# A two-part kernel (chunked delta rule, then PReLU feed-forward): reordering the second chunk's two steps, and starting the third block inversion earlier

## The chip, the cores and the metric

One core of a Trainium2 chip. TensorE (PE) multiplies into PSUM, VectorE (DVE), ScalarE (ACT) and GpSimd (POOL) work on SBUF tiles, SyncE (SP) issues nearly all DMAs. The metric is the device time of one execution in microseconds. Four runs of the kernel before took 666.1, 666.4, 667.12 and 671.37 us; their median is 666.76 us.

## The reference

```python
B, H, S, D = 4, 8, 768, 48
k_n = k / (norm(k) + 1e-06)
for t in range(S):                       # state: (B, H, D, D), zero at first
    y[:, :, t] = q_t @ state
    v_old = state^T k_t
    state += beta_t * outer(k_t, v_t - v_old)
x = y as (B*S, H*D)                      # 3072 x 384
h = x @ w_in                             # 384 x 2048
g = max(h, 0) + alpha * min(h, 0)
out = g @ w_out                          # 2048 x 384
```

All of it is float32. The first part is a recurrence over 768 tokens, the second a feed-forward layer over 3072 rows.

## The kernel before

**Steps.** The sequence is cut into 12 chunks of 64 tokens, and the four batches into two pairs. A step n is one chunk of one pair, so there are 24 steps, and steps 2c and 2c+1 make chunk c. The 128 partitions hold 64 tokens of two batches. For a step the kernel needs the Gram matrix of its keys (grams, L418), the inverse of a triangular 64x64 matrix for each head, and then the products with the running state: through_state (L754), solve (L785), outputs (L797) and next_state (L811). to_ffn (L833) turns the step's rows for the feed-forward layer.

**Before a step.** load_early (L139) brings a step's keys into one of three key buffers (a fourth at the start is lent by k_late). squares (L343) squares them on ACT and sums them on DVE; weigh (L352) takes the root on ACT, the reciprocal on DVE and two small products on POOL; flips (L383) transposes keys or queries on PE and copies them out on ACT. grams writes its products with weights by two DVE instructions (L430) into the tiles same and right, and keep (L467) copies half of right to same, on POOL for nearly all steps up to 9 and on ACT from step 10.

**The inverse.** Four steps are inverted together. turn_in (L492) transposes their Gram blocks by four DVE transposes (L489). eliminate (L501) then clears one triangle on POOL (L506, L510) and does 30 elimination steps on DVE, two instructions each (L516, L522), and back (L528) transposes the results by eight L489 into the tiles turned and inverse. That inverts the 32x32 blocks: 39 pieces, and four more where turn_in is part of it. The 64x64 inverse is put together in each step: place (L622) copies to diag and inv on ACT (L642, L648, and L659 for weights), between_1 (L702) and between_2 (L716) are the two products. For the first four steps 16x16 blocks are inverted first and joined by cross (L582), a generator of two halves: the first is 64 small matmuls (L593) and an ACT copy (L598) for a step, the second 96 (L603, L610) and three DVE instructions (L617, L619).

**The feed-forward layer.** ffn_in(c) (L922) makes 8 groups of 12 matmuls (L931) for chunk c, 48 parts in all; after each group ACT makes the negative part (L941) and DVE two instructions (L943). Two PSUM tiles, p_ffn, take turns. ffn_out(c) (L961) has 32 parts (L974). Both weights are converted at the start from words fetched into staging space: L209 fetches, L225 and L226 on ACT and L235 and L240 on DVE convert.

**Order.** The order of every engine is written out by hand: what the program issues first runs first on its engine, and an instruction that waits holds up all that stands behind it on that engine. weave (L1290) interleaves generators in equal shares, so that a feed-forward pass runs between the small products of the steps. The parts of the program around the change are, in order:

- first_chunk (L1417), steps 0 and 1; at its end it issues the loads of the late keys and values of steps 2 to 4, and fetches of weights.
- second_pair (L1555), steps 2 and 3, beside ffn_in(0) and 22 pieces of the conversion; alongside (L1552) issues so many parts of the one and pieces of the other. It also does squares, flips, weigh and grams of steps 4 to 7.
- A weave (L1628) of ffn_in(1), the conversion, statics (L1463: squares, weigh, flips, grams of steps 8 and 9) and the first 15 pieces of eliminate(1), the second inversion.
- A weave (L1637) of ffn_out(0), the last pieces of conversion and the rest of eliminate(1).
- Three parts of ffn_out(1), then prelude (L1642, step 4 made ready) and catch_up (L1654, grams of steps 10 and 11, flips and weights of 11 and 12) beside eight parts of ffn_out(1).
- attention(4) and attention(5) (L1307), each beside 11 parts of ffn_out(1) and 13 pieces of eliminate(2), the third inversion (L1697). turn_in(2) is issued all at once by keep(11) (L478).
- From step 6 on (L1712) each step has three stretches (L1691), whose shares of the next inversion stand in PIECES_OF and TURNS.

Of the kernel before, what the change touches and what calls it, by code (L numbers as in the profile page):

```python
# [43 lines left out]
def kernel(  # L44
# [363 lines left out]
    def now(pieces):  # L408
        for x in pieces:
            x()  # L410
# [56 lines left out]
    def keep(n):  # L467

        m, j = n // NJ, n % NJ
        for t in range(2):  # L470
            own = slice(64 * t + HB, 64 * t + C)
            if n < FIRST + NJ and n != NJ - 1:
                nc.gpsimd.tensor_copy(out=same[m][own, j], in_=right[n % EARLY][own, 1:])
            elif n < NJ and t == 0:
                nc.vector.tensor_copy(out=same[m][own, j], in_=right[n % EARLY][own, 1:])
            else:
                nc.scalar.copy(same[m][own, j], right[n % EARLY][own, 1:])
        if j == NJ - 1 and m in (0, 2):  # L478
            for _ in turn_in(m):
                pass  # L480

# [18 lines left out]

    def eliminate(m):  # L501

        if m not in (0, 2):
            yield from turn_in(m)
        r = block[m]
        nc.gpsimd.affine_select(  # L506
# [115 lines left out]
    def place(n, parts=(0, 1, 2, 3), by_vector=False):  # L622
        for _ in placing(n, parts, by_vector):
            pass
# [927 lines left out]
    def alongside(products, pieces, *gens):  # L1552
        weave((part(first_in, products), products), (part(convert_on, pieces), pieces), *gens)

    def second_pair():  # L1555

        n = 2
        both, x = (n, n + 1), NJ
        halves = [cross(0, slice(i * H, i * H + H), edge, half_way) for i in both]
        squares(x)  # L1560
        alongside(4, 2)
        for h in halves:
            next(h)
        flips(x, n)
        load_early(x + NKE)
        load_q(n + 2)
        squares(x + 1)
        alongside(5, 2)
        next(halves[0])
        flips(x + 1, n + 1)  # L1570
        load_early(x + 1 + NKE)
        load_q(n + 3)
        now(weigh(x))
        place(n, (0,))
        alongside(4, 2)
        next(halves[1])
        now(weigh(x + 1))
        place(n + 1, (0,))
        alongside(4, 2)
        for i in both:  # L1580
            now(between_1(i))
        now(grams(x))
        squares(x + 2)
        alongside(7, 3, (chain(*(placing(i, (1, 2, 3)) for i in both)), 6))
        for i in both:
            now(between_2(i))
        now(grams(x + 1))
        for i in both:
            scale_v(i)
        flips(x + 2, N)  # L1590
        load_early(x + 2 + NKE)
        now(weigh(x + 2))
        alongside(5, 3)
        y = ps_big()
        pieces = []
        for i in range(2):
            pieces += through_state(n + i, None, y[:, :, i * G * D : (i + 1) * G * D])
        now(pieces)
        squares(x + 3)
        alongside(5, 3)  # L1600
        y = ps_big()
        pieces = []
        for i in range(2):
            pieces += solve(n + i, y[:, :, i * G * D : (i + 1) * G * D])
        now(pieces)
        now(grams(x + 2))
        flips(x + 3, N)
        load_early(x + 3 + NKE)
        now(weigh(x + 3))
        alongside(5, 2)  # L1610
        pieces = []
        for i in both:
            y = ps_big()
            pieces += outputs(i, y[:, :, 0 : G * D]) + next_state(i, y[:, :, G * D : 2 * G * D])
        now(pieces)
        for i in both:
            load_late(i + 2)
            load_v(i + 3)
        alongside(5, 2)
        for i in both:  # L1620
            to_ffn(i)
        now(grams(x + 3))
        alongside(IN_PARTS - 44, 1)

    second_pair()
    fetch_out(len(stages))
    blocks, SOON, LAST = eliminate(1), 15, 6
    weave(  # L1628
        (part(conv_out, PARTS_OUT - 10 - LAST), PARTS_OUT - 10 - LAST), (ffn_in(1), IN_PARTS - 4),
        (statics(2 * NJ, FIRST + 3), 2 * (FIRST + 4 - 2 * NJ) + 1), (part(blocks, SOON), SOON),  # L1630
    )
    flips(FIRST + NJ, NJ)
    flips(N, NJ + 1)
    prep(FIRST + NJ)
    load_early(FIRST + NJ + NKE)
    load_q(NJ + 2)
    weave(  # L1637
        (conv_out, OUT_PARTS // 2), (part(blocks, WHOLE + PIECES - SOON), WHOLE + PIECES - SOON),
        (ffn_out(0, True), OUT_PARTS),
    )  # L1640

    def prelude(n):  # L1642
        place(n, (0,))
# [7 lines left out]
        place(n + 1, (0,))  # L1651
        yield

    def catch_up():  # L1654
        for n in range(FIRST + NJ, EARLY + NJ):
            now(grams(n))
            flips(n + 1, N)
            squares(n + 1)
            yield
            now(weigh(n + 1))  # L1660
            load_early(n + 1 + NKE)
            yield

    late = ffn_out(1)
    few, rest = OUT_PARTS // 4, 11
    for _ in part(late, OUT_PARTS - few - 2 * rest + 1):
        pass
    weave((prelude(NJ), 3), (catch_up(), 2 * (EARLY - FIRST), 0.1), (part(late, few), few))

    def feed_forward():  # L1670
        for c in range(2, FAST_IN):
# [22 lines left out]
        gens += [(part(blocks, share), share, 0.3), (each(later), len(later), soon)]  # L1694
        weave(*[x for x in gens if x[1] > 0])

    blocks, share = eliminate(2), WHOLE // 3  # L1697
    for n in range(NJ, JOINED):
        extra = [] if n == NJ else [(weight_sums(0, 0, 3), 3)]
        weave(  # L1700
# [3 lines left out]
        )  # L1704

    assert next(late, None) is None
    PIECES_OF = {JOINED: (2, 3, 2 * PIECES), JOINED + 1: (4, 4, 7)}
    TURNS = [(3, 3, 4), (3, 3, 4), (4, 4, 4), (0, 5, 6)]
    FILL = {JOINED: (8, 12, 12), JOINED + 1: (10, 12, 10), JOINED + 2: (8, 10, 12)}
    FILLS = [(12, 10, 12), (12, 18, 12)]  # L1710
# [78 lines left out]
```

## Time and profile before

| what | us |
|---|---|
| median of four runs | 666.76 |
| the profiled execution's own time | 669.61 |
| its span, first to last instruction | 667.9 |
| PE busy | 646.4 |
| DVE busy | 492.2 |
| ACT busy | 264.3 |
| mean granted clock of PE | 0.995 |

The profile is of one execution. A row of its timeline has the start, the duration, the engine, the line of the kernel, the operation and tiles, and the idle time before it with what ended that idle time. Matmuls are pipelined: the end of one is modelled, so that the time from the start of one burst to the start of the next tells what a burst costs, and the busy time says somewhat too much. SPq is the queue of DMA issues on SP; "issue" is time in which the engine waited for nothing that the profile shows.

### The profile page before, as it was taken

The numbers are of one execution on the slowest core, as the hardware profiler recorded it, in microseconds if no ns is written. First come the engines' busy times: TensorE is split into PE (matmuls) and PEld (weight loads), VectorE is DVE, ScalarE is ACT, GpSimd is POOL, SyncE is SP. The second block draws the span as 40 slices with busy tenths as digits, with TensorE's granted clock in tenths as the row PEclk, the third lists the DMA queues.
The fourth block names the chain that finished last, engine by engine and source line by source line (L and its number), as shares of the span: only waits on it lengthen the run. The fifth ranks groups of instructions, "written<-read, shape, count | busy, mean of one in ns | idle before, by whom it ended". The sixth has DMA issues, their size and how long they took to land.

```text
span 667.9 us, 22126 instructions
## 1 busy us (share of the span) xinstructions
PE 646.4 (97%) x9551; PEld 571.4 (86%) x9551; DVE 492.2 (74%) x1180; ACT 264.3 (40%) x621; POOL 93.9 (14%) x201
## 2 busy tenths in 40 slices
PE   5998899999899999999999999999999999999997
PEld 4577788666578998998998998998999999999997
DVE  4946789878899859747959747859869658568283
ACT  4926667325445334334334333223234235042140
POOL 6000212101010100001000000000035034053260
PEclk9979999999999999999999999999999999999999
DMA  7837664201342032022022022112112210100000
GB/s 120 244 80 200 148 189 128 72 25 38 59 88 42 13 70 50 13 62 49 15 49 37 14 50 37 19 45 37 27 37 38 36 35 6 26 14 2 24 1 25
DMA packets 110962, 37.72 MB, mean 56 GB/s; under 512 B 104160, under 2 KB 107248, under 8 KB 110864
## 3 DMA queue, kind: packets, MB, share of 16 engines
q1 hardware_dynamic: 109088, 35.81, 24.7%
q8 instruction: 75, 1.23, 0.8%
q10 hardware_dynamic: 1776, 0.49, 0.4%
q14 instruction: 23, 0.19, 0.1%
HBM read 31.56 MB, written 4.72 MB: 54 GB/s over the span
## 4 chain that ended last, share of the span: by engine, by line
PE 86%; DVE 7%; ACT 2%; issue 1%; DMA 1%; SPq 1%; ACTq 0%; DVEq 0%
PE p_ffn L931 22%; PE p_ffn L996 17%; PE p_more L1248 8%; PE p_more L1164 4%; PE p_ffn L974 4%; PE p_ffn L1154 3%; PE p_ffn L1248 3%; PE p_pair L377 3%; PE p_ffn L1159 2%; PE p_pair L788 2%; PE p_pair L763 2%; PE p_pair L801 2%; PE p_pair L674 2%; PE p_pair L1392 2%; PE p_pair L424 1%
## 5 line engine op out<-in xcount | busy, mean ns | idle before, releaser
L931 PE MATMUL p_ffn<-xt,w_in 128*128 128x256 f32 x768 | 175.1, 382 | 3.6 <-ACT beside L400 1.5
L931 PEld LDWEIGHTS p_ffn<-xt,w_in 128*128 128x128 f32 x768 | 142.7, 190 | 24.0 <-ACT beside L400 1.9
L943 DVE SCALAR_TENSOR_TENSOR act<-act,al_t,p_ffn 128x256 f32<-128x256 f32 x112 | 48.6, 475 | 30.4 <-ACT act L941 30.3
L941 ACT ACTIVATE act<-p_ffn 128x512 f32<-128x512 f32 x56 | 33.3, 595 | 81.8 <-PE p_ffn L931 81.7
L522 DVE TENSOR_TENSOR block<-block,prod 128x30 f32<-128x30 f32 (+9 forms) x150 | 49.9, 333 | 5.1
L1188 POOL TENSOR_TENSOR k_t<-k_t 128x128 f32<-128x128 f32 (+1 forms) x48 | 29.5, 615 | 166.6 <-ACT k_t L1183 164.1
L516 DVE TENSOR_TENSOR prod<-block 128x30 f32<-128x30 f32 (+9 forms) x150 | 48.9, 326 | 1.8
L996 PE MATMUL p_ffn<-w_out,act 128*128 128x192 f32 x288 | 49.6, 328 | 0.1
L996 PEld LDWEIGHTS p_ffn<-w_out,act 128*128 128x128 f32 x288 | 46.5, 190 | 0.8 <-issue 0.5
L366 POOL TENSOR_TENSOR beta_t<-beta_t,rec 128x8 f32<-128x8 f32 x24 | 6.4, 268 | 286.9 <-DVE rec L364 267.0
L842 ACT COPY xt<-p_pair 128x384 f32<-128x384 f32 x22 | 10.4, 476 | 90.7 <-PE p_pair L840 76.9
L1188 POOL TENSOR_TENSOR block<-block 128x128 f32<-128x128 f32 (+1 forms) x48 | 27.9, 582 | 16.7 <-ACT block L1183 14.2
L1154 PE MATMUL p_ffn<-xt,w_in 128*128 128x256 f32 x96 | 28.7, 380 | 0.0
L792 DVE TENSOR_TENSOR u<-p_pair,wgt 128x384 f32<-128x384 f32 x24 | 13.2, 556 | 14.7 <-PE p_pair L674 14.0
L773 DVE TENSOR_TENSOR r<-v_raw,p_pair 64x192 f32<-64x192 f32 (+1 forms) x66 | 23.2, 352 | 1.1
L686 ACT COPY inv<-p_pair 32x256 f32<-32x256 f32 x40 | 14.4, 360 | 23.8 <-DVE u L792 23.6
L1202 DVE SCALAR_TENSOR_TENSOR act<-block,al_t,act 128x256 f32<-128x256 f32 x32 | 19.1, 638 | 5.2 <-ACT block L1198 5.1
L1016 DVE TENSOR_TENSOR o_sb<-u,p_ffn 128x192 f32<-128x192 f32 x24 | 7.9, 352 | 20.2 <-PE p_ffn L996 19.8
L1248 PE MATMUL p_more<-w_out,act 128*128 128x192 f32 x128 | 21.8, 329 | 0.0
L349 DVE TENSOR_REDUCE norm<-ksq 128x8 f32<-128x384 f32 x24 | 13.0, 545 | 12.0 <-ACT ksq L347 11.9
L642 ACT ACTIVATE inv<-inverse,which 128x256 f32<-128x256 f32 x44 | 21.6, 504 | 0.3
L1183 ACT COPY k_t<-p_more 128x512 f32<-128x512 f32 x16 | 9.4, 585 | 30.6 <-PE p_more L1164 25.9
(224 smaller groups left out, 1422.0 us busy)
## 6 DMA issues: line engine op xcount, KB each, us to landing
w_out<-in_moe_w_in_dram SPq DMA_DIRECT2D x12, 512.0 KB, 5.7
qp<-in_q_dram SPq DMA_DIRECT2D x48, 96.0 KB, 3.1
v_raw<-in_v_dram SPq DMA_DIRECT2D x48, 96.0 KB, 3.1
kl<-in_k_dram SPq DMA_DIRECT2D x96, 48.0 KB, 2.7
out_dram<-o_sb SPq DMA_DIRECT2D x92, 48.0 KB, 1.6
space_out<-in_moe_w_out_dram SPq DMA_DIRECT2D x11, 384.0 KB, 3.7
ke<-in_k_dram SPq DMA_DIRECT2D x43, 96.0 KB, 3.5
w_out<-in_moe_w_out_dram SPq DMA_DIRECT2D x5, 384.0 KB, 4.4
```

The lines of the kernel that those rows point to most:

```text
L516: nc.vector.tensor_tensor(out=prod, in0=r[:, 0:j, j : j + 1].to_broadcast([128, j, n]), in1=r[:, j : j + 1, j + 1 : HB].to_broadcast([128, ...
L522: nc.vector.tensor_tensor(out=r[:, 0:j, j + 1 : HB], in0=r[:, 0:j, j + 1 : HB], in1=prod, op=ALU.add)
L773: nc.vector.tensor_tensor(out=r[to, a], in0=v_in[to, a], in1=p[own, a, :, 0:D], op=ALU.subtract)
L931: nc.tensor.matmul(p_h[:, i], w_in[:, t, (f + i) * 128 : (f + i + 1) * 128], xt[:, t], start=(t == 0), stop=(t == KT - 1),)
L941: nc.scalar.activation(g, p_h, ACT.Relu, scale=-1.0)
L943: nc.vector.scalar_tensor_tensor(out=g[:, i], in0=g[:, i], scalar=al_t[:, f + i : f + i + 1], in1=p_h[:, i], op0=ALU.mult, op1=ALU.add,)
L974: nc.tensor.matmul(p_o[u], gs[f // 2][:, f % 2, u * 128 : (u + 1) * 128], w_out[:, f], start=(f == 0), stop=(f == FT - 1),)
L996: nc.tensor.matmul(p, x(i), w(i), start=(i == 0), stop=(i == FP - 1))
L1154: nc.tensor.matmul(p[:, f * 256 : f * 256 + 256], w(2, f), xt[:, 2], start=True, stop=False)
L1164: nc.tensor.matmul(q[:, j], a, b, start=True, stop=True)
L1188: nc.gpsimd.tensor_tensor(out=dst, in0=a, in1=b, op=ALU.add)
L1248: nc.tensor.matmul(p, x(i), w(i), start=(i == 0), stop=(i == FP - 1))
```

## The change

second_pair is written anew: the same calls, in another order. The two steps' halves, between products, through_state, solve and outputs no longer stand together for both steps, but one after the other, with a few feed-forward parts behind each. squares of steps 6 and 7 and grams of steps 4 to 7 are issued earlier, weigh and flips of steps 6 and 7 too. The first 7 pieces of eliminate(1) are issued near the end of second_pair (`rows`): the four of turn_in, the POOL piece and two elimination steps. The second weave takes 13 pieces more, where it had 15.

Steps 10 and 11 move: their flips, squares, weights, loads and grams are issued in the third weave, by statics, and catch_up does the flips, squares and weights of step 12 alone. turn_in(2) is no longer issued by keep but is part of eliminate(2), which begins beside the three parts of ffn_out(1) (four pieces), goes on in the prelude's weave (six), in attention(4) and attention(5) (nine each in place of thirteen), and ends in step 6 (3, 4 and 8 pieces; 2, 3 and 8 before). eliminate(3) has one piece in place of four in step 7's first stretch, and three more in step 8.

```diff
--- before.py
+++ after.py
@@ -475,7 +475,7 @@
                 nc.vector.tensor_copy(out=same[m][own, j], in_=right[n % EARLY][own, 1:])
             else:
                 nc.scalar.copy(same[m][own, j], right[n % EARLY][own, 1:])
-        if j == NJ - 1 and m in (0, 2):
+        if (m, j) == (0, NJ - 1):
             for _ in turn_in(m):
                 pass
 
@@ -500,7 +500,7 @@
 
     def eliminate(m):
 
-        if m not in (0, 2):
+        if m > 0:
             yield from turn_in(m)
         r = block[m]
         nc.gpsimd.affine_select(
@@ -1554,90 +1554,94 @@
 
     def second_pair():
 
-        n = 2
-        both, x = (n, n + 1), NJ
-        halves = [cross(0, slice(i * H, i * H + H), edge, half_way) for i in both]
+        n, m, x = 2, 3, NJ
+        halves = [cross(0, slice(i * H, i * H + H), edge, half_way) for i in (n, m)]
+
+        def rows(k):
+            return part(blocks, k), k
+
         squares(x)
         alongside(4, 2)
-        for h in halves:
-            next(h)
+        next(halves[0])
+        alongside(2, 1)
+        next(halves[1])
         flips(x, n)
         load_early(x + NKE)
         load_q(n + 2)
         squares(x + 1)
-        alongside(5, 2)
+        alongside(4, 2)
         next(halves[0])
-        flips(x + 1, n + 1)
+        flips(x + 1, m)
         load_early(x + 1 + NKE)
         load_q(n + 3)
         now(weigh(x))
         place(n, (0,))
-        alongside(4, 2)
+        squares(x + 2)
+        alongside(3, 2)
         next(halves[1])
         now(weigh(x + 1))
-        place(n + 1, (0,))
-        alongside(4, 2)
-        for i in both:
-            now(between_1(i))
-        now(grams(x))
-        squares(x + 2)
-        alongside(7, 3, (chain(*(placing(i, (1, 2, 3)) for i in both)), 6))
-        for i in both:
-            now(between_2(i))
-        now(grams(x + 1))
-        for i in both:
-            scale_v(i)
+        place(m, (0,))
+        alongside(2, 1)
         flips(x + 2, N)
         load_early(x + 2 + NKE)
+        now(grams(x))
+        squares(x + 3)
+        alongside(2, 1)
+        now(between_1(n))
         now(weigh(x + 2))
-        alongside(5, 3)
-        y = ps_big()
-        pieces = []
-        for i in range(2):
-            pieces += through_state(n + i, None, y[:, :, i * G * D : (i + 1) * G * D])
-        now(pieces)
-        squares(x + 3)
-        alongside(5, 3)
-        y = ps_big()
-        pieces = []
-        for i in range(2):
-            pieces += solve(n + i, y[:, :, i * G * D : (i + 1) * G * D])
-        now(pieces)
-        now(grams(x + 2))
+        alongside(3, 1, (placing(n, (1, 2, 3)), 3))
+        now(between_1(m))
+        now(grams(x + 1))
+        alongside(4, 1, (placing(m, (1, 2, 3)), 3))
+        now(between_2(n))
+        scale_v(n)
         flips(x + 3, N)
         load_early(x + 3 + NKE)
         now(weigh(x + 3))
-        alongside(5, 2)
-        pieces = []
-        for i in both:
+        alongside(3, 2)
+        now(between_2(m))
+        scale_v(m)
+        now(grams(x + 2))
+        alongside(3, 2)
+        y = ps_big()
+        now(through_state(n, None, y[:, :, 0 : G * D]))
+        alongside(2, 1)
+        now(through_state(m, None, y[:, :, G * D : 2 * G * D]))
+        now(grams(x + 3))
+        alongside(3, 1)
+        y = ps_big()
+        for i in range(2):
+            now(solve(n + i, y[:, :, i * G * D : (i + 1) * G * D]))
+            alongside(2 + i, 1, rows(2))
+        for i in (n, m):
             y = ps_big()
-            pieces += outputs(i, y[:, :, 0 : G * D]) + next_state(i, y[:, :, G * D : 2 * G * D])
-        now(pieces)
-        for i in both:
+            now(outputs(i, y[:, :, 0 : G * D]) + next_state(i, y[:, :, G * D : 2 * G * D]))
             load_late(i + 2)
             load_v(i + 3)
-        alongside(5, 2)
-        for i in both:
+            alongside(2, 1, *([rows(1)] if i == n else []))
+        for i in (n, m):
             to_ffn(i)
-        now(grams(x + 3))
-        alongside(IN_PARTS - 44, 1)
-
+        alongside(IN_PARTS - 44, 1, rows(2))
+
+    blocks, BEGUN, SOON, LAST = eliminate(1), 7, 13, 6
     second_pair()
     fetch_out(len(stages))
-    blocks, SOON, LAST = eliminate(1), 15, 6
     weave(
         (part(conv_out, PARTS_OUT - 10 - LAST), PARTS_OUT - 10 - LAST), (ffn_in(1), IN_PARTS - 4),
         (statics(2 * NJ, FIRST + 3), 2 * (FIRST + 4 - 2 * NJ) + 1), (part(blocks, SOON), SOON),
     )
-    flips(FIRST + NJ, NJ)
-    flips(N, NJ + 1)
-    prep(FIRST + NJ)
-    load_early(FIRST + NJ + NKE)
+    for i in range(2):
+        flips(N, NJ + i)
     load_q(NJ + 2)
+    n = WHOLE + PIECES - BEGUN - SOON
     weave(
-        (conv_out, OUT_PARTS // 2), (part(blocks, WHOLE + PIECES - SOON), WHOLE + PIECES - SOON),
+        (conv_out, OUT_PARTS // 2), (part(blocks, n), n),
+        (statics(FIRST + NJ, EARLY + 3), 2 * (EARLY + 4 - FIRST - NJ) + 1),
         (ffn_out(0, True), OUT_PARTS),
     )
+    for _ in blocks:
+        assert False
+    blocks = eliminate(2)
 
     def prelude(n):
         place(n, (0,))
@@ -1651,21 +1655,22 @@
         place(n + 1, (0,))
         yield
 
-    def catch_up():
-        for n in range(FIRST + NJ, EARLY + NJ):
-            now(grams(n))
-            flips(n + 1, N)
-            squares(n + 1)
-            yield
-            now(weigh(n + 1))
-            load_early(n + 1 + NKE)
-            yield
+    def catch_up(n):
+        flips(n, N)
+        squares(n)
+        yield
+        now(weigh(n))
+        load_early(n + NKE)
+        yield
 
     late = ffn_out(1)
     few, rest = OUT_PARTS // 4, 11
-    for _ in part(late, OUT_PARTS - few - 2 * rest + 1):
-        pass
-    weave((prelude(NJ), 3), (catch_up(), 2 * (EARLY - FIRST), 0.1), (part(late, few), few))
+    n = OUT_PARTS - few - 2 * rest + 1
+    weave((part(late, n), n), (part(blocks, PIECES), PIECES))
+    weave(
+        (prelude(NJ), 3), (catch_up(EARLY + NJ), 2, 0.1), (part(late, few), few),
+        (part(blocks, 6), 6),
+    )
 
     def feed_forward():
         for c in range(2, FAST_IN):
@@ -1694,7 +1699,7 @@
         gens += [(part(blocks, share), share, 0.3), (each(later), len(later), soon)]
         weave(*[x for x in gens if x[1] > 0])
 
-    blocks, share = eliminate(2), WHOLE // 3
+    share = 9
     for n in range(NJ, JOINED):
         extra = [] if n == NJ else [(weight_sums(0, 0, 3), 3)]
         weave(
@@ -1704,7 +1709,10 @@
         )
 
     assert next(late, None) is None
-    PIECES_OF = {JOINED: (2, 3, 2 * PIECES), JOINED + 1: (4, 4, 7)}
+    PIECES_OF = {
+        JOINED: (3, WHOLE - 2 * PIECES - 6 - 2 * share - 3, 2 * PIECES),
+        JOINED + 1: (1, 4, 7), JOINED + 2: (4, 4, 5),
+    }
     TURNS = [(3, 3, 4), (3, 3, 4), (4, 4, 4), (0, 5, 6)]
     FILL = {JOINED: (8, 12, 12), JOINED + 1: (10, 12, 10), JOINED + 2: (8, 10, 12)}
     FILLS = [(12, 10, 12), (12, 18, 12)]
```

## The prediction

> **What bounds the kernel now.** I read the page's first part, then the busy time of each engine stage by stage (stages cut where the PE timeline shows the code's stages begin), then who TensorE waited for in the two stretches where it is not full, then single rows.
>
> ```profile
> span 667.9 us, 22126 instructions
> PE 646.4 (97%) x9551; PEld 571.4 (86%) x9551; DVE 492.2 (74%) x1180; ACT 264.3 (40%) x621; POOL 93.9 (14%) x201
> ```
>
> TensorE (PE) is the bound. Only its idle time can be won, plus what the page counts as busy because a burst's modelled end overhangs a wait (about 0.27 us a wait).
>
> ```profile
> 51.44:97.53 46.09, 42.41 (x1023) 36.41 (x1024) 32.53 (x80) 29.47 (x68) 6.73 (x16) 1.00 0.72 182
> 97.53:122.33 24.80, 24.59 (x180) 20.93 (x179) 23.16 (x66) 16.24 (x34) 4.80 (x11) 1.00 0.43 110
> 122.33:142.98 20.65, 20.65 (x67) 12.12 (x66) 17.55 (x52) 4.66 (x11) 0.78 (x2) 1.00 0.17 39
> 142.98:154.22 11.24, 11.24 (x159) 6.71 (x157) 6.02 (x14) 6.84 (x17) 0.41 (x2) 1.00 0.23 54
> 154.22:168.40 14.18, 13.83 (x291) 9.62 (x290) 12.44 (x36) 8.19 (x24) 1.79 (x4) 1.00 0.19 38
> 168.40:183.93 15.53, 13.60 (x289) 9.30 (x288) 14.33 (x35) 6.68 (x19) 0.55 (x2) 1.00 0.33 59
> 183.93:199.76 15.83, 14.29 (x274) 12.32 (x273) 14.36 (x39) 7.66 (x21) 1.69 (x4) 1.00 0.47 90
> 199.76:218.02 18.26, 16.92 (x232) 14.51 (x228) 17.98 (x40) 9.38 (x24) 0.80 (x1) 1.00 0.24 44
> ```
>
> Columns: length, then PE, weight loads, DVE, ACT, POOL busy, granted clock, DMA share, GB/s. The rows are second_pair; the second weave (ffn_in(1)); the third (ffn_out(0)); the prelude; attention(4); attention(5); step 6; step 7. PE idles 3.7 us in the first and 5.2 us in the last four; after 218 it is never idle. DVE is nearly full in the second weave and from attention(5) on.
>
> ```profile
> PE p_pair L424 <- issue: 1.4, 1, 1.4
> PE p_pair L610 <- issue: 1.2, 2, 1.0
> PE p_pair L377 <- DVE inv L729: 0.9, 1, 0.9
> ```
>
> ```profile
> PE p_ffn L931 <- ACT beside L400: 1.5, 1, 1.5
> PE p_ffn L931 <- DVE act L943: 1.2, 1, 1.2
> PE p_pair L788 <- DVE a_t L444: 1.1, 2, 0.8
> PE p_pair L801 <- DVE u L792: 0.7, 1, 0.7
> ```
>
> The first three are waits in 51.4 to 97.6 (2.6 us with no releaser), the others in 143 to 218: there DVE runs late. One pair of rows shows how late: step 6's r is made 5 us after PE began its product.
>
> ```profile
> 183.93 1.00 PE L763 MATMUL p_pair<-beside,k_t 48*64 48x112 f32 x32
> 188.88 1.08 DVE L773 TENSOR_TENSOR r<-v_raw,p_pair 128x192 f32<-128x192 f32 x3
> ```
>
> **The change, part by part.** All times are on the scale of the profiled execution (669.61 us, of which the span is 667.9); it lies 2.9 above the median 666.76 of the four runs shown, and I take the difference over to the median.
>
> *A. second_pair.* No product is added. PE's work by start-to-start times in its timeline: a feed-forward part (two L931 matmuls) 0.444, 48 of them 21.3; cross 3.4 (L593 1.39 for both steps, L603/L610 1.0 each); six flips 2.6; between_1 and between_2 3.9; four grams 2.5; through_state with query 2.5; solve 1.1; outputs with next_state 2.1; to_ffn 0.7: 40.1 of 46.1, so 6.0 is lost and could be won. The finer weaving puts 0.9 to 1.8 us of L931 behind each small product, which covers a copy (0.5) or an update on DVE (0.4 to 0.6).
>
> What is late next is squares(7). It moves from after through_state(2) to before between_1(2), and needs the load of step 7's keys.
>
> ```profile
> 64.89 1.31 SPq L137 DMA_DIRECT2D ke<-in_k_dram x2
> DMA to landing us min/median/max: 7.3/7.3/7.3
> 84.08 0.54 ACT L347 ACTIVATE ksq<-ke 128x384 f32<-128x384 f32 x1
> ```
>
> The load leaves SP at 64.9 behind kl, v_raw and three space_out pieces that first_chunk already queued, so nothing in second_pair makes it earlier; 7.3 us later, at 72.1 (second half about 72.6), it has landed. Now squares(7) runs at 84 and meets no wait. After the change I follow ACT in its own order: squares(4), L598, the L225/L226 pairs (1.3 each), L941 (0.5), k_t and q copies (0.48 each), weigh(4), place(2), squares(6), weigh(5), place(3), flips(6)'s copy: it reaches squares(7) at about 65.7 and stands until 72.6, some 7 us. Queued behind it are L225/L226 of the last w_in piece (1.3), between_1(2)'s copy (0.4), weigh(6) (0.5), L941 (0.5) and place(2,(1)) (0.4); between_2(2) needs the last, so it starts at 72.6+0.5+3.1=76.2. PE, which waits for none of this until then, reaches it at 71.0 by work alone, up to 73.6 with the 2.6 us of issue waits above: a new wait of 2.6 to 5.2. From there PE has 20.8 us (between_2 twice 2.0, flips(7) 0.4, 24 parts 10.7, grams 1.2, and 6.5 for the rest), ending at 97.0 to 97.6, as now.
>
> DVE is worse off. Its reduce(7) and reciprocal(6) stand in line too, so it idles until 75.3 with 21.9 us to do before step 3's y: L235/L240 4.8, L943 4.0 (0.8 a pair), L430 2.0, r and masked 3.4, u 1.0, updates 1.9, L729 and scale_v 1.8, four turn_in transposes of inversion 1 2.4 (moved in here), reciprocals and waits on ACT 0.6. That gives 97.2; one wait for an L941 queued behind place(3) makes it 97.7. to_ffn(3) then starts at 97.8, and the last four parts end at 99.9 against 97.5: **+2.4**. Bounds: -3.6 if no squares wait shows (6.0 less twelve short waits of 0.2), +5.8 if the clock falls (rival 2).
>
> The granted clock bears on this: between 42 and 48 it was 0.50 (6.8 us in all, 3.4 us lost), after 1.07 us of idle in 36 to 40. The Trainium skill (TensorE: Matmul & The Clock Gate, What's actually happening) puts the drop after one idle window of about 3.4 us; it speaks against this change, because the new wait may be that long, and the sum by it would be 3.4 higher. The skill's DMA: Bandwidth & Descriptors (Anatomy of one DMA) gives, for loads issued by POOL, about 2.0 us plus bytes over 436 GB/s, 2.2 us as an estimate for 96 KB; by that the keys are there at 67.8, the wait is 4.8 shorter, and the sum 4.8 lower. The trace's 7.3 us behind a full queue (DMA share 0.90 from 64.8 to 66.3) decides.
>
> SP: the loads for steps 9 and 10 leave earlier (77.9 for the second, now 87.9), 96 KB each into queues that are idle from 76 to 80. POOL's keep(7) (two L473, 0.8) stands before the first transpose, but u(2) and L943 lie between. Both cost nothing; if keep(7) were late, a transpose holds up u(3) on DVE one for one. Separate PSUM tiles for y are the same banks in turn.
>
> *B. Second weave.* Inversion 1 has 13 pieces here, not 15: pieces 7 to 19 (updates j=3 to 15, 9.9 us by L516/L522 rows) in place of four transposes (2.4) and j=1 to 10 (6.5). DVE goes from 24.7 to 25.7 while PE has 24.3. A lag of about 1.2 us is free (two p_ffn banks, one group 2.66, less L941 and L943); it was 1.4 at the start. I take **+0.7** between 0 and +1.5.
>
> *C. Third weave and steps 10, 11.* flips, squares, weigh, loads and grams of steps 10 and 11 move beside ffn_out(0). PE there: 20.65+2*0.44+2*0.62=22.8. DVE sheds j=11 to 15 (4.2) and takes one more squares and weigh and four L430: 19.8, under PE, so inversion 1 ends with the weave and not 3.2 us after it. ACT (4.7 of 20.7 busy) takes keep's copies. turn_in(2), which keep(11) issued at once, becomes four pieces beside three parts.
>
> *D. Prelude, attention(4), attention(5).* Inversion 2 begins in the prelude: 6 pieces there, then 9 and 9 where 13 and 13 stood. DVE against PE: 6.3 to 8.8, 12.2 to 13.1, 15.3 to 12.5 (before: 12.7 and 18.5 in the two attentions). Following both in order from the end of the third weave, step 6 begins 36.0 us later, where ideal PE is 34.4 and the present time 40.9. Less what C adds to PE, from 121.0 it begins at 180.7, not 183.9: **-3.2**, plus +0.7 for short waits I can't place.
>
> *E. Steps 6 and 7.* Step 6 takes two more updates (1.6), but r lags 3.7, not 5.0, so the 1.5 wait (L931 behind ACT's L477 behind L430) shrinks: **-1.2**. Step 7's first stretch has one piece for four (three transposes, 1.8, go to step 8, where DVE has room: 14.0 of 20 busy at 240 to 260): the wait of 1.2 goes, **-1.2**. C to E together -4.9, between -7 (all idle of the last four rows and their overhang) and -1 (DVE's lag remains).
>
> Sum: +2.4+0.7-4.9=-1.8: span 666.1, this execution 667.8, on the median 665.0.
>
> **Rivals.** *1. The keys come in time* (landing by 68, or ACT arrives later): A is -3.6 and the sum -7.8: 659.0. For it: the 6 us are there, mostly under bursts that now get cover. Against: the landing row. *2. The clock falls* in the new wait, after about 74: half speed for 6.8 us costs 3.4; it decides for slower once more than 1.8 of it isn't covered by DVE's backlog. Sum +1.6: 668.4. For it: the fall at 42 after less idle. Against: L931 is dense work, and DVE is the later one there. *3. The relief does nothing*: DVE still trails in attention(5) (15.3 to 12.5) and in-order waits for weigh eat the rest; C to E give 2.0: +1.1, 667.9.
>
> **How the numbers follow.** Forecast 0.45 (662 to 667), rival 1 0.22 (655 to 662), rival 2 0.18 (666 to 673), rival 3 0.15 (666 to 670). The range 657.5 to 671 leaves about 0.1 on either side. About 1% (6.7 us) is what a measurement can tell: faster by more (under 660.1) is two thirds of rival 1 and a tail, 0.17; slower (over 673.4) a tail of rivals 2 and 3, 0.07; the rest 0.76.
>
> **What would show it.** A: ACT idle of 5 to 7 us before an L347, released by a ke load; PE idle before an L722; DVE dense from 75 on; the second weave starting near 100. C, D: L489 of inversion 1 ending with ffn_out(0); fewer L788/L801 waits. E: no 1.2 wait at L931. Wrong if squares(7) meets no wait, or the clock shows 0.5 after 60.

## The result and the profile after

The changed kernel takes 670.34 us (median of 54 runs, 666.18 to 678.21), the kernel before 668.12 us (median of 78 runs). The ratio is 1.0038, with a 95% interval of 1.0026 to 1.0051: 2.5 us slower (1.7 to 3.4), where 1.8 us faster was forecast. The ratio leaves out the slowest 3 of the 54 runs; the two medians differ by 2.2 us. The time lies inside the stated range of 657.5 to 671 and under the 1% that the prediction took as the least a measurement can tell, but the interval is clear of no change and on the other side of it. The profiled execution after has a time of 670.86 us of its own and this head:

```profile
span 669.1 us, 22128 instructions
PE 649.6 (97%) x9551; PEld 572.4 (86%) x9551; DVE 492.3 (74%) x1180; ACT 264.7 (40%) x621; POOL 93.6 (14%) x201
```

PE is busy 3.2 us longer with the same 9551 matmuls: some of them ran slower. The busy times stage by stage, for the same eight stages as before (columns: stretch and length, PE, weight loads, DVE, ACT, POOL busy, granted clock, DMA share, GB/s):

```profile
49.91:101.48 51.57, 46.69 (x1023) 38.03 (x1024) 35.90 (x88) 29.82 (x67) 7.20 (x18) 0.93 0.64 165
101.48:126.35 24.87, 24.81 (x182) 21.00 (x180) 23.27 (x67) 16.59 (x35) 3.40 (x8) 1.00 0.43 112
126.35:149.51 23.16, 22.96 (x134) 13.41 (x133) 19.92 (x57) 7.28 (x18) 1.01 (x4) 1.00 0.20 44
149.51:158.78 9.27, 9.27 (x91) 5.37 (x90) 4.93 (x16) 5.47 (x15) 2.03 (x4) 1.00 0.31 65
158.78:172.47 13.69, 13.69 (x291) 9.62 (x290) 9.79 (x25) 6.56 (x17) 0.00 (x0) 1.00 0.13 29
172.47:185.91 13.44, 13.26 (x288) 9.32 (x287) 12.41 (x31) 6.24 (x18) 0.61 (x2) 1.00 0.34 59
185.91:200.29 14.38, 14.36 (x273) 12.33 (x273) 13.15 (x37) 8.07 (x22) 1.76 (x4) 1.00 0.56 104
200.29:218.53 18.24, 16.75 (x232) 14.67 (x228) 17.91 (x39) 9.30 (x23) 0.00 (x0) 1.00 0.25 45
```

The second row to the seventh do what the change meant: the two attentions and step 6 have next to no idle PE left. The first does not: second_pair takes 51.6 us, its clock is 0.93 on average, and PE is idle for 4.9 us. The table sets the lengths side by side, each stage cut at the start of its first matmul (the first row was cut 0.05 us later here, and 0.2 us later for the kernel before); the last column is the same kernel with one call moved (experiment 1).

| stretch, us | before | after | after, squares(7) later |
|---|---|---|---|
| up to second_pair | 51.4 | 49.9 | 48.4 |
| second_pair | 45.9 | 51.5 | 45.0 |
| second weave | 25.0 | 24.9 | 24.9 |
| third weave | 20.6 | 23.2 | 23.2 |
| prelude | 11.3 | 9.3 | 9.3 |
| attention(4) | 14.2 | 13.7 | 13.7 |
| attention(5) | 15.5 | 13.4 | 13.4 |
| steps 6 and 7 | 34.1 | 32.6 | 32.6 |
| the rest | 449.9 | 450.6 | 450.5 |

The first line is no effect of the change: that code is the same in all kernels here, and it took 47.4 to 51.4 us from one execution to the next. From second_pair on, after is 2.7 us longer: +5.6, -0.1, +2.5, -2.0, -0.5, -2.1, -1.5 and +0.7.

Where the 5.6 us come from is seen in three views. First ACT in the timeline, then DVE, with the idle time and what ended it in brackets, and the time that the loads of keys took in that stretch:

```profile
70.69 0.52 ACT L347 ACTIVATE ksq<-ke 128x384 f32<-128x384 f32 x1 [5.41 <-DMA ke<-in_k_dram]
73.47 0.50 ACT L642 ACTIVATE diag<-inverse,which 128x256 f32<-128x256 f32 x1
```

```profile
71.24 0.55 DVE L349 TENSOR_REDUCE norm<-ksq 128x8 f32<-128x384 f32 x1 [5.33 <-ACT ksq L347]
```

```profile
L137 SPq DMA_DIRECT2D ke<-in_k_dram x6: 596/756/2871, 62.6 to 73.2; - x6
DMA to landing us min/median/max: 3.1/4.3/7.7
```

ACT stands 5.4 us before squares(7), since step 7's keys (two loads of 96 KB, the first issued at 62.6; theirs is the 7.7 in the last line) land from 70.3 on; DVE stands behind it, and step 2's piece of place (the L642 at 73.47) is queued behind it on ACT. Then PE:

```profile
68.93 1.99 PE L931 MATMUL p_ffn<-xt,w_in 128*128 128x256 f32 x8
74.02 1.92 PE L722 MATMUL p_pair<-diag,mid 64*64 64x32 f32 x32 [3.09 <-ACT diag L642]
75.86 1.10 PE L377 MATMUL p_pair<-ident,ke 128*112 128x128 f32 x4
76.75 2.77 PE L931 MATMUL p_ffn<-xt,w_in 128*128 128x256 f32 x6
```

PE waits 3.1 us for that L642, and what follows is slow: six L931 take 2.77 us, where eight took 1.99 before the wait. Four slices of 3.41 us show why (the column after POOL is the granted clock):

```profile
69.66:73.07 3.41, 1.26 (x6) 0.76 (x4) 0.89 (x2) 2.32 (x7) 0.00 (x0) 1.00 0.41 74
73.07:76.49 3.42, 2.47 (x35) 2.41 (x36) 2.68 (x7) 3.35 (x12) 0.98 (x4) 0.50 0.58 108
76.49:79.90 3.41, 3.41 (x18) 2.40 (x17) 2.62 (x7) 3.17 (x8) 0.96 (x3) 0.50 0.24 41
79.90:83.31 3.41, 3.41 (x91) 2.91 (x93) 2.50 (x6) 1.74 (x4) 0.77 (x2) 1.00 0.94 330
```

In the slice that holds most of the wait PE was busy 1.26 us; for the next two the clock is 0.50. So the wait is paid twice, once as idle time and once as 6.8 us at half speed.

### The profile page after: what moved, and what is told of

It reads as the page before. It is cut to its first block, busy times and chain, and to the rows that moved or that the text cites. A ratio compares the mean times of both kernels' runs of the same rounds, so it can differ in the third digit from the quotient of the medians.

```text
span 669.1 us, 22128 instructions
## 1 busy us (share of the span) xinstructions
PE 649.6 (97%) x9551; PEld 572.4 (86%) x9551; DVE 492.3 (74%) x1180; ACT 264.7 (40%) x621; POOL 93.6 (14%) x201
## 4 chain that ended last, share of the span: by engine, by line
PE 82%; DVE 11%; ACT 3%; DMA 2%; issue 1%; SPq 0%; ACTq 0%; DVEq 0%
PE p_ffn L931 19%; PE p_ffn L996 17%; PE p_more L1248 8%; PE p_ffn L974 5%; PE p_more L1164 4%; PE p_ffn L1154 3%; PE p_ffn L1248 3%; PE p_ffn L1159 2%; PE p_pair L377 2%; PE p_pair L763 2%; PE p_pair L674 2%; PE p_pair L788 2%; PE p_pair L424 2%; DMA ke<-in_k_dram 2%; PE p_pair L801 2%; DVE act L943 1%
## 5 line engine op out<-in xcount | busy, mean ns | idle before, releaser
L931 PE MATMUL p_ffn<-xt,w_in 128*128 128x256 f32 x768 | 178.4, 386 | 2.7 <-DVE act L943 2.0
L931 PEld LDWEIGHTS p_ffn<-xt,w_in 128*128 128x128 f32 x768 | 142.8, 191 | 23.7 <-issue 3.1
L943 DVE SCALAR_TENSOR_TENSOR act<-act,al_t,p_ffn 128x256 f32<-128x256 f32 x112 | 48.6, 475 | 28.0 <-ACT act L941 27.8
L941 ACT ACTIVATE act<-p_ffn 128x512 f32<-128x512 f32 x56 | 33.3, 595 | 84.0 <-PE p_ffn L931 83.9
L522 DVE TENSOR_TENSOR block<-block,prod 128x30 f32<-128x30 f32 (+9 forms) x150 | 49.9, 333 | 5.2
L1154 PE MATMUL p_ffn<-xt,w_in 128*128 128x256 f32 x96 | 28.7, 380 | 0.0
L773 DVE TENSOR_TENSOR r<-v_raw,p_pair 64x192 f32<-64x192 f32 (+1 forms) x66 | 23.3, 353 | 2.6 <-PE p_pair L763 1.6
L752 ACT COPY y<-p_pair 128x384 f32<-128x384 f32 x22 | 10.5, 479 | 30.7 <-PE p_pair L748 29.1
L763 PE MATMUL p_pair<-beside,k_t 48*64 48x112 f32 x704 | 21.7, 259 | 0.5 <-issue 0.3
L974 PE MATMUL p_ffn<-w_out,act 128*128 128x384 f32 x64 | 21.7, 490 | 0.2 <-ACT w_out L225 0.2
```

The lines of the kernel that those rows point to most:

```text
L522: nc.vector.tensor_tensor(out=r[:, 0:j, j + 1 : HB], in0=r[:, 0:j, j + 1 : HB], in1=prod, op=ALU.add)
L763: nc.tensor.matmul(p[half(t ^ a), a, g], k_t[n][dims(a), g, half(t)], beside[bp][dims(a), t, g])
L931: nc.tensor.matmul(p_h[:, i], w_in[:, t, (f + i) * 128 : (f + i + 1) * 128], xt[:, t], start=(t == 0), stop=(t == KT - 1),)
L941: nc.scalar.activation(g, p_h, ACT.Relu, scale=-1.0)
L943: nc.vector.scalar_tensor_tensor(out=g[:, i], in0=g[:, i], scalar=al_t[:, f + i : f + i + 1], in1=p_h[:, i], op0=ALU.mult, op1=ALU.add,)
L974: nc.tensor.matmul(p_o[u], gs[f // 2][:, f % 2, u * 128 : (u + 1) * 128], w_out[:, f], start=(f == 0), stop=(f == FT - 1),)
```

## The experiments

The theory: squares(7) stands too early in ACT's queue, the wait for its load reaches PE through place(2), and PE's wait brings the clock down; the rest of the change is a gain. Rivals: the new order itself costs the time (finer weaving, pieces of inversion 1 on DVE), or the fall of the clock has nothing to do with the wait. Every ratio below is to the kernel before.

**1. squares(7) later.** The kernel after, with one call moved down:

```diff
         now(grams(x))
-        squares(x + 3)
         alongside(2, 1)
...
         flips(x + 3, N)
+        squares(x + 3)
         load_early(x + 3 + NKE)
```

> The changed kernel with one call moved: step 7's squares stand after flips(7) instead of before between_1(2). Theory: squares(7) makes ACT stand 5.4 us for keys still on their way, PE then waits 3.1 us and its clock is halved for 6.8 us; without it ACT never waits for a ke load here, the clock stays 1.0 after 46, second_pair falls from 51.6 to 44 to 46 us, and the time is 0.990 to 0.994 of before. Rival, the finer weaving and the seven pieces of inversion 1 load DVE too much: second_pair stays at 49 us or more, ratio 1.000 or above.

Measured: ratio to before 0.9963 (0.994 to 0.9987), second_pair 45.0; the stage came out as expected, the gain in time smaller. ACT meets no wait for the keys, PE none before L722, and the clock stays at 1.00. The stage's row and the row of PE that had waited, in this run:

```profile
48.42:93.47 45.05, 43.58 (x1023) 35.80 (x1024) 35.59 (x88) 29.70 (x67) 7.21 (x18) 1.00 0.70 182
```

```profile
69.41 1.12 PE L722 MATMUL p_pair<-diag,mid 64*64 64x32 f32 x32
70.94 1.46 PE L931 MATMUL p_ffn<-xt,w_in 128*128 128x256 f32 x6
```

The same 32 matmuls take 1.12 and not 1.92, the six L931 1.46 and not 2.77. The new order with its pieces of inversion 1 takes 45.0 us, 0.9 less than the old: the order is not what costs. It doesn't win much either. PE is idle for 1.5 us in place of 3.7, but busy for 43.6 in place of 42.4 with the same products: the 48 feed-forward parts, now in 17 bursts and not in 10, take 23.4 us from start to start, where they took 22.1.

**2. squares(7) early in the kernel before.** The converse, one call moved up in the kernel before:

```diff
         place(n + 1, (0,))
+        squares(x + 3)
         alongside(4, 2)
...
         now(pieces)
-        squares(x + 3)
```

> The kernel before with that call alone moved forward: squares(7) directly after place(3), all else in the old order. Theory: ACT stands 4 to 6 us for the keys, which land at about 72 whatever second_pair does, PE waits 2 to 4 us before between_2, and if its clock falls second_pair grows from 46.1 to 50 or 52; ratio 1.004 to 1.009, and 1.002 to 1.004 if the clock holds. Rival, the finer weaving is what costs: 1.000.

Measured: 1.0104 (1.0069 to 1.0139), second_pair 50.6 (+4.7), with a longer wait of PE (5.9 us) and a higher ratio than expected. In the timeline and in slices of PE's clock:

```profile
74.33 3.51 PE L722 MATMUL p_pair<-diag,mid 64*64 64x32 f32 x61 [5.87 <-ACT diag L642]
```

```profile
66.84:70.25 3.41, 1.61 (x8) 1.08 (x6) 0.31 (x1) 0.87 (x2) 0.00 (x0) 1.00 1.05 123
70.25:73.66 3.41, 0.00 (x0) 0.00 (x0) 3.38 (x9) 3.35 (x8) 0.79 (x2) 1.00 0.43 81
73.66:77.08 3.42, 2.75 (x52) 2.76 (x54) 1.36 (x4) 3.19 (x10) 0.00 (x0) 0.50 0.00 0
```

The single call brings wait and fall into the old order as well. A slice with PE busy for 1.61 of 3.41 us was not followed by a fall; the next, with none, was.

**3. squares(7) half way.** The kernel after, squares(7) directly before between_1(3):

```diff
         alongside(3, 1, (placing(n, (1, 2, 3)), 3))
+        squares(x + 3)
         now(between_1(m))
```

(and taken away where it stood).

> The changed kernel with step 7's squares only some instructions later on ACT: behind between_1(2)'s copy, weigh(6), a group's L941 and the three copies of place(2), ahead of between_1(3)'s copy. ACT still meets it before the keys land. Theory: what matters is what stands behind the waiting instruction; between_2(2) now has all it needs, PE works on, ACT waits 1 to 3 us, PE 0 to 1, the clock holds, second_pair takes 45 to 47 us, ratio 0.995 to 0.999. Rival, any wait of ACT there passes to PE: PE waits 2 us or more and the clock falls again, ratio 1.002 or more.

Measured: 0.9941 (0.991 to 0.9971), second_pair 46.0. ACT still waits for the keys, but with step 2's pieces of place ahead of it:

```profile
ACT ksq L347 <- DMA ke<-in_k_dram: 1.3, 1, 1.3
```

PE waits for none of it. So ACT's wait, here of 1.3 us, costs nothing of itself; what stands behind it in the queue decides.

**4. The load earlier.** The kernel after, where three fetches of w_out are issued behind the key loads of steps 7 and 8 and no longer ahead of them:

```diff
 first_chunk(mask, convert)
-fetch_out(SPACES)
...
         load_q(n + 3)
+        fetch_out(SPACES)
```

> The changed kernel with squares(7) where the change put it, but the three fetches of w_out words (384 KB each), which stood on SP ahead of the keys of step 7, issued behind the loads for steps 7 and 8. Theory: the keys are late because of what lies ahead of them in the queue; they then land at about 66 and not at 70.3, ACT waits 0 to 1.5 us in place of 5.4, PE does not wait before between_2(2), the clock holds, and second_pair falls from 51.6 to 45 to 47 us; ratio to before 0.993 to 0.998. Rival, such a load takes 7 us here whatever is ahead of it: ACT waits 3.5 us or more and the ratio is 1.000 to 1.004.

Measured: 0.9961 (0.9939 to 0.9983), second_pair 45.5, clock 1.00. The keys, issued at 60.2, land at 65.8, after 5.6 us:

```profile
66.06 0.52 ACT L347 ACTIVATE ksq<-ke 128x384 f32<-128x384 f32 x1 [2.49 <-DMA ke<-in_k_dram]
```

ACT's wait is a little longer than expected (2.5 us, 0 to 1.5 expected), and PE has none. squares(7) stands in its early place here: with its keys some microseconds sooner, the early call costs PE nothing.

**5. Filling the wait with idle products.** The kernel after, with seven products whose results nothing uses, into free columns of a PSUM tile, before between_2(2):

```diff
+        free = big[-1][:, 0, 256:512]
         alongside(4, 1, (placing(m, (1, 2, 3)), 3))
+        for _ in range(7):
+            nc.tensor.matmul(
+                free, ident, k_late[0].rearrange("p h d -> p (h d)")[:, 0:256]
+            )
         now(between_2(n))
```

> The changed kernel with seven extra matmuls of 256 columns (3.1 us of PE time, results unused) issued before between_2(2), where PE waits 3.1 us for ACT. It separates the wait from the clock. Theory: the wait stays, but PE is busy in it, the clock stays at 1.0, and second_pair falls from 51.6 by 2 to 3.4 us to 48.2 to 49.6; ratio to before 0.999 to 1.001. Rival, the halved clock was hidden behind DVE's backlog, as the prediction had it: second_pair stays at 51 to 52, ratio 1.003 to 1.005.

Measured: 1.0125 (1.0088 to 1.0162), second_pair 56.5. It missed its aim. In the view of PE's waits:

```profile
PE p_pair L1598 <- DVE right L430: 5.4, 1, 5.4
```

The idle products had to wait themselves, for DVE to have read the columns beside theirs in the same tile, and DVE stood behind squares(7). The clock fell at 73.2 and was back at 80.04, as the products ended. So this run doesn't separate the wait from the clock. One number is of use: from the first matmul of between_2(2) to the end of second_pair this run took 24.07 us, at full clock. In experiment 1 it is 24.06, in the kernel after 27.46.

**6. Filling the wait with feed-forward parts.** Five numbers changed in the kernel after, so that six parts of ffn_in(0) stand before between_2(2) and no longer behind it:

```diff
-        alongside(4, 1, (placing(m, (1, 2, 3)), 3))
+        alongside(10, 1, (placing(m, (1, 2, 3)), 3))
         now(between_2(n))
...
-        alongside(3, 2)
+        alongside(1, 2)
         now(between_2(m))
...
-        alongside(3, 2)
+        alongside(1, 2)
...
-        alongside(2, 1)
+        alongside(1, 1)
...
-        alongside(3, 1)
+        alongside(2, 1)
```

> The kernel after, with squares(7) where the change put it, so that ACT still waits 4.5 to 5.5 us for step 7's keys. Only TensorE is given work for that time: six parts of ffn_in(0) (six by 0.444, 2.7 us) stand before between_2(2) that stood behind it, two each from the first two groups of three, one each from the next two. Theory (the fall of the clock near 73 us comes from TensorE's wait of 3.1 us before between_2(2), and the fall is what made second_pair 3.4 us longer still): TensorE waits under 1.0 us there, the granted clock is 1.0 from 55 us to the end of second_pair, second_pair takes 46.0 to 48.5 us instead of 51.5, of which more than 46.0 is what ACT and DVE are late. Rival one (the fall has nothing to do with the wait and comes in this stretch anyway, as the early one comes at random): clock 0.5 near 73 without a wait, second_pair 49.5 to 52. Rival two (the parts can't run ahead, since ACT in its wait doesn't drain their PSUM tiles): TensorE waits 2 us or more at an L931 in place of the L722, the clock falls, second_pair 51 to 54. Ratio to the kernel before by the theory 0.994 to 1.000.

Measured: 1.0078 (1.0046 to 1.011), second_pair 54.0: rival two. PE, DVE and ACT in the timeline:

```profile
67.67 1.99 PE L931 MATMUL p_ffn<-xt,w_in 128*128 128x256 f32 x8
74.87 5.28 PE L931 MATMUL p_ffn<-xt,w_in 128*128 128x256 f32 x12 [5.21 <-DVE act L943]
```

```profile
73.85 0.87 DVE L943 SCALAR_TENSOR_TENSOR act<-act,al_t,p_ffn 128x256 f32<-128x256 f32 x2 [0.28 <-ACT act L941]
```

```profile
70.94 0.52 ACT L347 ACTIVATE ksq<-ke 128x384 f32<-128x384 f32 x1 [7.16 <-DMA ke<-in_k_dram]
73.24 0.58 ACT L941 ACTIVATE act<-p_ffn 128x512 f32<-128x512 f32 x1
```

The extra parts open a new group, whose PSUM tile L943 must have read; that needs the L941 at 73.24, and this stands behind squares(7) on ACT too. The clock fell at 73.0 for 6.8 us. squares(7) began 23.0 us after the stage did, against 20.8 in the kernel after, which makes up for nearly all of the 2.5 us more. Here the wait can't be covered by work that ACT has to drain. Whether the clock holds when PE is kept busy in the wait was thus not seen in either attempt; that the two belong together rests on the runs in which the wait is gone.

**7. The old second_pair.** The kernel after with before's second_pair, and inversion 1 in the shares that belong to it:

```diff
-    blocks, BEGUN, SOON, LAST = eliminate(1), 7, 13, 6
+    blocks, BEGUN, SOON, LAST = eliminate(1), 0, 15, 6
```

> The changed kernel with second_pair as it was before; inversion 1 has 15 pieces in the second weave and 28 in the third, everything later is as changed. Theory: second_pair takes 46 us again and the later stages keep their gain of about 3.5 us (from 126.3 to 200.3 in the changed kernel against 122.3 to 199.8 before); ratio 0.993 to 0.996. Rival, that gain needs the seven pieces done in second_pair: inversion 1 ends 4 us after the third weave, attention(4) and (5) wait for DVE again, ratio 0.998 to 1.001.

Measured: 0.9949 (0.9918 to 0.998). Every stage behind the second weave is as short as in the kernel after (third weave 23.0, prelude 9.4, attentions 13.7 and 13.4, steps 6 and 7 32.6): that gain doesn't hang on second_pair. By the ratio this kernel can't be told from experiment 1, so nothing here shows that the new order of second_pair, freed of its wait, is better than the old. The old second_pair took 48.1 us in this execution, for another reason. Its waits, and the clock around them:

```profile
PE p_pair L610 <- issue: 2.0, 1, 2.0
PE p_pair L424 <- issue: 1.5, 1, 1.5
```

```profile
53.88:57.29 3.41, 1.41 (x98) 1.26 (x97) 1.87 (x5) 1.20 (x3) 0.00 (x0) 1.00 0.42 72
57.29:60.70 3.41, 3.41 (x15) 3.06 (x13) 0.85 (x4) 1.43 (x5) 0.00 (x0) 0.50 0.53 91
```

The waits without a releaser stand at the same lines as in the kernel before (1.0 and 1.4 there). Here the slice with the first of them was followed by a fall of the clock for 3.4 us.

**8. The old end of inversion 3.** Experiment 1 and before's shares for steps 7 and 8:

```diff
-        JOINED + 1: (1, 4, 7), JOINED + 2: (4, 4, 5),
+        JOINED + 1: (4, 4, 7),
```

> The kernel with step 7's squares moved behind flips(7) (ratio 0.9963), with the shares of inversion 3 in steps 7 and 8 as before the change: four transposes in step 7's first stretch, not one. The prediction took 1.2 us off for that part. Theory now: the three transposes stood behind the L943 that PE waits for, so the wait of 1.5 us in step 7 stays between 1.2 and 1.8 and the time is the same within 0.5 us. Rival, as predicted: the wait grows by 1.2 us or more and the time with it.

Measured: 0.9961 (0.9931 to 0.9991). Step 7's wait at L931 is 1.5 us with three transposes more or less; steps 6 and 7 take 32.9 (+0.3), the rest 449.9 (-0.7). The kernel after has a wait in step 8 that is gone here:

```profile
261.61 0.67 PE L931 MATMUL p_ffn<-xt,w_in 128*128 128x256 f32 x2 [0.48 <-DVE act L943]
```

**9. Step 7's first stretch freed altogether.** Experiment 1, with no piece of inversion 3 in that stretch and its weight sum (L918, L885) in the next:

```diff
-        JOINED + 1: (1, 4, 7), JOINED + 2: (4, 4, 5),
+        JOINED + 1: (0, 4, 8), JOINED + 2: (4, 4, 5),
...
-            extra[0] = [(weight_sums(1, 3, 4), 1), (placing(n + 1, (1, 2, 3)), PLACING)]
+            extra[0] = [(placing(n + 1, (1, 2, 3)), PLACING)]
+            extra[1] = [(weight_sums(1, 3, 4), 1)]
```

> The kernel with step 7's squares moved behind flips(7), and in step 7 nothing of DVE's optional work ahead of the L943 that PE waits for: no piece of inversion 3 in the first stretch (0, 4, 8 in place of 1, 4, 7) and the last weight sum (L918, 0.9 us) issued in the second stretch. Theory: that L943 is late by the DVE queue ahead of it, so the wait of 1.5 us falls to 0 to 0.3 and step 7 from 18.2 to about 17.0 us; ratio 0.993 to 0.996. Rival, the lag comes from step 6's transposes and the wait stays above 1 us: 0.9963 as without.

Measured: 0.9929 (0.9895 to 0.9963); the wait is gone, steps 6 and 7 take 31.2. The piece and the weight sum were moved together, so that their shares aren't separated.

**10. The same, with inversion 3 ending in step 7.**

```diff
-        JOINED + 1: (0, 4, 8), JOINED + 2: (4, 4, 5),
+        JOINED + 1: (0, 8, 7),
```

> The kernel after with squares(7) late and with step 7's first stretch free of pieces of the third inversion and of its weight sum (as in the run step7_light), but the third inversion now ends in step 7 as before the change (0, 8 and 7 pieces there, none in step 8; step 8 has its old shares). Theory (what step 7 sheds to step 8 costs 0.7 us behind step 7, since the end of the program has less cover; step 7 itself waits only in its first stretch, where DVE is full): the wait before L931 stays away, steps 6 and 7 together 31.2 to 31.6 us, the rest from 449.8 to 450.0 instead of 450.5, ratio to the kernel before 0.990 to 0.993. Rival (the eight pieces of the second stretch bring the wait back, later in step 7): steps 6 and 7 together 32.5 or more with a PE wait behind DVE in step 7, and nothing won over step7_light, ratio 0.993 to 0.996.

Measured: 0.9936 (0.9912 to 0.996), median 660.88 us, steps 6 and 7 31.2, the rest 449.8. The wait stays away and step 8's is gone too, as expected. By the stages behind step 7 it is 0.7 us under experiment 9, which the ratios can't tell apart. Both beat the kernel before, and by their ratios to it the kernel after.

## Why the prediction was right or wrong

*Point by point, from second_pair on.* The way to the wait came out as written: keys 20.4 us after the stage began (20.7 to 21.2 forecast), ACT idle 5.4 (7), PE idle 3.1 before an L722 (2.6 to 5.2), between_2(2) 24.1 after the beginning (24.8). Without the clock, second_pair would be 51.5-3.4=48.1, 2.2 more than before; the term was +2.4. That these two agree is in part luck: the forecast had PE done in time and DVE 2.4 late, and what was late is PE's own work, which had been put too low.

*The step that failed* is the judgement on rival 2, that the fall "decides for slower once more than 1.8 of it isn't covered by DVE's backlog", and against it that "DVE is the later one there". The fall came (the prediction's own sign of being wrong, a clock of 0.5 after 60), and nothing of it was covered. From between_2(2) to the end of the stage, in the kernel after and in experiment 1:

```profile
74.02:101.48 27.46, 25.67 (x507) 20.80 (x508) 22.85 (x56) 13.56 (x31) 4.87 (x11) 0.89 0.47 133
69.41:93.47 24.06, 22.59 (x508) 18.53 (x508) 21.14 (x52) 11.99 (x26) 4.69 (x10) 1.00 0.61 167
```

The difference is the whole 3.4. (DVE isn't late in experiment 1, so this alone doesn't settle what its backlog would have covered; its waits, shown below, do.) Two things were wrong in that step. PE's work from there was put at 20.8; experiment 1 has PE busy for 22.6 and waiting 1.5 more, so that PE has no slack of three microseconds behind DVE. The largest part of the difference is in the 24 feed-forward parts, put at 10.7: in nine short bursts they took 11.7 from start to start. (The same error made the best case of second_pair too good: with no wait for the keys it was to win 3.6 us, and experiment 1 won 0.9.) And DVE's backlog is no queue that runs by itself. In the kernel after it was gone by 79.5, and from there DVE waits for the slowed PE:

```profile
DVE inv L729 <- PE p_pair L722: 1.3, 1, 1.3
DVE u L792 <- PE p_pair L788: 1.0, 1, 1.0
DVE r L773 <- PE p_pair L763: 0.4, 1, 0.4
```

In experiment 1 none of these waits is there. An engine that is late but fed by the slowed one passes the delay on. The fall was likely, too. Of the 54 runs of the kernel after, 2 had a mean granted clock of 0.999 or more, and of the 19 runs of experiments 2, 5 and 6, where PE waits over 5 us, none; of the 63 runs of experiments 1, 3, 4, 8, 9 and 10, where PE doesn't wait there, 41 had. Averaged over the runs the clock was 0.992 in the kernel after and 0.997 in the 63, which by 668 us is 5.3 us lost against 1.8: the difference is 3.5. (The 54 runs weren't taken side by side with the 63. The kernel before, in 81 runs beside the experiments, had 0.995, or 3.4 us lost, and 29 runs at 0.999 or more, so part of what the experiments win over it may be fewer falls elsewhere, with causes that weren't tried.) Rival 2 had a chance of 0.18. With +1.6 for that rival, the sum would have been 668.4; +2.5 was measured.

The Trainium skill (TensorE: Matmul & The Clock Gate, What's actually happening) has a free-running window of 3413 ns; the changes of the clock in these traces, which lie whole numbers of 3.41 us apart within an execution, agree. Its "≥1 idle window" asks for more idle time than these rows do: PE was still busy for 1.26 and 1.41 of 3.41 us in the slices ahead of the falls in the kernel after and in experiment 7.

*B* (+0.7): -0.1. DVE was put at 25.7 us in the weave and is busy for 23.3, under PE's 24.8.

*C and D* (-3.2 and +0.7 for short waits): third weave to attention(5) 59.6 after and 61.6 before, -2.0 where -2.5 was forecast. Inversion 2's even shares do what was said: DVE 9.8 of 13.7 and 12.4 of 13.4 in the two attentions.

*E, step 6* (-1.2): -1.45. *E, step 7* (-1.2): nothing; its wait went from 1.2 to 1.5. This is the second step that failed. Of the four transposes in that stretch before, only the first stood ahead of the L943 for which PE waits; three behind it can't hold it up. DVE in the kernel before, then after, then PE after:

```profile
212.04 0.95 DVE L918 TENSOR_TENSOR w_out<-w_out,more 128x768 f32<-128x768 f32 x1
212.91 0.68 DVE L885 TENSOR_TENSOR sums<-sums,act 128x512 f32<-128x512 f32 x1
213.51 0.67 DVE L489 STREAM_TRANSPOSE block<-same 128x256 f32<-128x256 f32 x1
214.07 0.83 DVE L943 SCALAR_TENSOR_TENSOR act<-act,al_t,p_ffn 128x256 f32<-128x256 f32 x2
214.82 0.66 DVE L489 STREAM_TRANSPOSE block<-same 128x256 f32<-128x256 f32 x1
```

```profile
212.87 0.95 DVE L918 TENSOR_TENSOR w_out<-w_out,more 128x768 f32<-128x768 f32 x1
213.74 0.69 DVE L885 TENSOR_TENSOR sums<-sums,act 128x512 f32<-128x512 f32 x1
214.34 0.66 DVE L489 STREAM_TRANSPOSE block<-same 128x256 f32<-128x256 f32 x1
214.90 0.83 DVE L943 SCALAR_TENSOR_TENSOR act<-act,al_t,p_ffn 128x256 f32<-128x256 f32 x2
```

```profile
215.87 2.83 PE L931 MATMUL p_ffn<-xt,w_in 128*128 128x256 f32 x12 [1.49 <-DVE act L943]
```

The weight sum (1.6 us) and the first transpose (0.6) stand ahead in both; taking those out ended the wait (experiment 9).

*Not foreseen:* +0.7 behind step 7. The pieces that went to step 8 "where DVE has room" met a 0.5 us wait there; experiments 8 and 10, without them, have the 0.7 back. The forecast went by an average: in the kernel after DVE is busy for 14.6 of the 20 us from 240 to 260, but for 10.7 of the 12 from 250 to 262, where the wait is.

*What stays open.* Whether PE kept busy through the wait would have kept its clock. Why PE stands for 1 to 2 us without a releaser at L610 and L424, more in one execution than in the next, was not tried; nor what takes the clock down early in some executions.

## What to carry to other kernels

Before an instruction that depends on a load is moved forward on an in-order engine, follow everything queued behind it up to the engine that sets the time: here two loads of 96 KB of keys held up a copy that TensorE needed, and also the copies that would have let TensorE do other work (experiment 6). In second_pair waits of 2.0, 3.1 and 5.2 to 5.9 us were followed by a lowered clock, and none of 1.5 or less was: price a wait that long as the wait plus half of the time at the lowered clock, which here lasted 3.4 or 6.8 us, and count a cover only if the covering engine doesn't itself wait for TensorE. When work is taken off an engine to end a wait, look up which instructions stand ahead of the releasing one in its queue; those behind it were worth nothing here.

## What the runs showed of the hardware

The clock falls at the edge of slices of 3.41 us, counted alike through an execution (after: 38.94 and 73.07 are ten slices apart), and lasts one or two of them. In second_pair, slices with PE busy for 0.00 to 0.06, 1.26 or 1.41 us were followed by a fall, one with 1.61 was not; near the start, one with 1.71 (experiment 3) was. Where the edges lie differs between executions, so that a wait may be cut in two. In the executions profiled before and after, the clock also fell at 41.28 and 38.94, in code that is the same in all these kernels and that kept its clock there in the others (two of them, experiments 3 and 7, had an early fall at 16.5 and 16.3); the slice ahead of the former had PE busy for 2.57 of 3.42 us, so idle time as the profile counts it is not all that decides.

A 96 KB load took 7.7 us from its issue behind the fetches of weights (after), and 5.6 us with three of them moved behind it (experiment 4).
